# A squared-ReLU attention with an MLP behind it: eight plain block products for the first two chunks, and the weights' sums made later

## Chip, core and metric

One core of one Trainium2 chip. The metric is the device time of one execution in microseconds (us), the median of the runs; lower is better. "PE" is TensorE, "DVE" is VectorE, "ACT" is ScalarE, "POOL" is GpSimd and "SP" is SyncE, which here only issues DMAs.

## What is computed

```python
# u, v: (4, 3008, 256); z: (4, 3008, 64); w_in: (256, 2048); w_out: (2048, 256)
scores = (1.0 / S) * np.matmul(z, z.transpose(0, 2, 1))
attn = np.maximum(scores, 0.0) ** 2
x = (u * np.matmul(attn, v)).reshape(12032, 256)
h = x @ w_in
g = h * np.clip(h + 3.0, 0.0, 6.0) / 6.0
out = g @ w_out
```

The two weights arrive as 64-bit floats; the kernel turns them into 32-bit floats itself.

## The kernel before

**Precision.** Each operand of a matmul is split into a rounded part ("hi", made by a copy on ACT) and the rest ("lo", a subtraction on DVE). A product is three matmuls: lo x hi, hi x lo and hi x hi.

**Attention.** There are 24 chunks of 512 tokens (the last of each batch has 448), and in each 12 pairs of key blocks, so 288 pairs, counted by `g`. A direct pair has 4 matmuls of scores, a mirrored pair has none: it reads a transposed tile that was stored earlier (`turn`, line 374, a DVE transpose). Then come 12 matmuls with `v` (`av`, line 525). The scores run two pairs ahead of `av`: in pair `g` the kernel makes `ah` and `al` of pair `g + 2` (`scores`, line 424). `square_on` says who squares the second copy of the scores: "aa" ACT alone, "dd" DVE alone, "da" half each.

**MLP.** It works on two chunks at a time (12 such couples, `i`), in 8 units each (`q`, 256 columns of `w_in`). Unit `m` starts at pair `g = 33 + 3m` (`MLP_FROM`, `EVERY`) and is spread over three pairs. `group` (line 692) projects up with seven block products by Strassen's scheme (in Winograd's form), 21 matmuls, with sums of blocks of `x` (`split_x`, line 568) and of `w_in` (`S1` to `S4`). It collects them in the PSUM banks `x` and `y`, the ones that the scores use too. Copies on ACT and additions on DVE put the results together, then come ReLU (ACT), `gate` (DVE) and the split into `gh` and `gl`. The unit's down projection is 24 matmuls (`downs_of`, line 623), issued during the next unit.

**The weights.** `weight_ops` (line 796) is a generator. For each of 16 weight blocks it fetches 512 KB, converts it with six DVE instructions (`to_f32`, line 136), makes for `w_in` four sums of blocks (`pieces`, line 171), lets ACT round them, subtracts (`finish`, line 198) and stores hi and lo in DRAM. A step runs up to its next `yield`; an "in" and an "out" block together have 20 steps. `build_rate` (line 816) sets the steps for each pair: 2 for pairs 2 and 3, 1 up to 11, 3 up to 17, 4 up to 32, then 5. `spare()` in the main loop takes one step at a time, at fixed places between the other instructions.

**Order.** The order of every queue is the order of the program (`manual_schedule`); each engine works through its own list and waits where an operand or a buffer isn't ready. `split_x(0)` runs one step a pair from pair 24 to 32; `fetch_unit` (line 687) loads a unit's weights by SP.

Of the kernel before, what the change touches and what calls it, by code (L numbers as in the profile page):

```python
# [15 lines left out]
P = 128  # L16
CH = 512
# [19 lines left out]


# [1 line left out]
def relu2_attention_then_hswish_mlp(  # L40
# [28 lines left out]
    def f(ap):  # L69
        return ap.bitcast(F32)  # L70
# [34 lines left out]
    def copy_later(out, of):  # L105
        copies.append((now, out, of))
# [61 lines left out]
    dw = {}  # L168
    early = True

    def pieces(kind, w):

        hi, lo = piece_tiles(kind)
        if kind == "out":
            copy_later(hi, w)
            return [(hi, lo, w)]
        s = stg.tile([P, 4, P], F32, tag="stg", name="s4")
        a11, a21 = w[:, 0, :P], w[:, 0, P:]
        a12, a22 = w[:, 1, :P], w[:, 1, P:]
        copy_later(hi[:, A11:A22], w[:, :, :P])  # L180
        copy_later(hi[:, A22], a22)
        add(s[:, 0], a21, a22)
        yield
        sub(s[:, 1], s[:, 0], a11)
        yield
        sub(s[:, 2], a11, a21)
        yield
        sub(s[:, 3], a12, s[:, 1])
        copy_later(hi[:, S1:], s)
        yield  # L190
        return [
            (hi[:, A11:A22], lo[:, A11:A22], w[:, :, :P]),
            (hi[:, A22], lo[:, A22], a22),
            (hi[:, S1:], lo[:, S1:], s),
            hi, lo,
        ]

    def finish(kind, q, parts):
        if kind == "out":
            hi, lo = parts[0][:2]  # L200
        else:
            *parts, hi, lo = parts
        flush_copies(upto=now)
        for h, l, of in parts:
            sub(l, of, f(h))
            yield
        d = dw[kind, q] = dwpool.tile([P, 2, *hi.shape[1:]], F32, tag=f"{kind}{q}", name=f"dw{kind}")
        for k, t in enumerate((hi, lo)):
            nc.sync.dma_start(out=d[:, k], in_=f(t))

    built = []

    def piece_tiles(kind):
        homes = (("wh", "wl"), ("gh0", "gl0"), ("gh1", "gl1")) if early else (("wh", "wl"),)
        tags = homes[len(built) % len(homes)]
        built.append(kind)
        tiles = []
        for tag in tags:
            if tag[0] == "g":
                t = gpool.tile([P, 2, CH], F32R, tag=tag, name=tag)  # L220
                t = t.rearrange("p r n -> p (r n)")
            else:
                t = wpool.tile([P, 7 * P], F32R, tag=tag, name=tag)
            if kind == "in":
                tiles.append(t[:, :7 * P].rearrange("p (m f) -> p m f", m=7))
            else:
                tiles.append(t[:, :2 * D].rearrange("p (r d) -> p r d", r=2))
        return tiles

    def fetch_w(kind, q):  # L230
        while (kind, q) not in dw:
            next(w_ops)
        shape = [P, 2, 7, P] if kind == "in" else [P, 2, 2, D]
        if kind == "in":
            t = wring.tile(shape, F32R, tag="wi", name="wi")
        else:
            t = opool.tile(shape, F32R, tag="wo", name="wo")
        nc.sync.dma_start(out=f(t), in_=dw[kind, q])
        return t

    vt, zt = {}, {}
# [326 lines left out]
    def split_x(i):  # L568


        raw = raw_x[i]
        n = tokens(i)[1] // 2
        left, right = raw[:, :, :n], raw[:, :, n:2 * n]
        new = xt[i] = {}

        def piece(k, src):
            shape = [P, 2, CH] if k < 3 else [P, CH]
            homes = ((xpool, f"xh{k}"), (xpool, f"xl{k}"))
            if i == NPR - 1:
# [9 lines left out]
            return lambda: sub(lo, src, f(hi))  # L589

        if i < NPR - 1:
            pool, tag = (rpool, "r") if i else (hpool, "hb")
            t = pool.tile([P, 2, CH], F32, tag=tag, name="t")[:, :, :n]
# [24 lines left out]
        yield  # L618
# [229 lines left out]
    with tc.manual_schedule():  # L848
# [13 lines left out]
        first_scores()  # L862
        run(second, 1)
        split_z(0, 1)
        g_done = 2
        to_fetch += [(b, c, p) for b, c, p in pairs if is_mirrored(b, c, p)]
        for i, (b, c) in enumerate(chunks):
            ahead = b + 1 if c == NCH - 1 and b + 1 < B else None
            for p in range(NPAIR):
# [171 lines left out]
    return a.reshape(2, -1).T.reshape(-1)  # L1041


def _orders():
# [13 lines left out]
    return of_u, of_y  # L1058
# [35 lines left out]
```

## Time and profile before

| | |
|---|---|
| median of 3 runs | 1823.61 us (1823.44 to 1826.42) |
| the profiled execution: its own time, and the span of its instructions | 1825.48 us, 1823.7 us |
| PE, weight loads, DVE, ACT busy | 99%, 87%, 83%, 66% of the span |
| granted TensorE clock | 1.000 (2.4 GHz) |
| DMA | 329.5 MB, mean 181 GB/s |

A matmul's record is about 0.38 us long, but the next one starts 0.22 us later: records overlap, and a PE that is "busy" may still have lost time. The time lost in a stretch is its length less the number of its matmuls times their distance. DVE and ACT records overlap their successors by some hundredths of a microsecond.

### The profile page before, as it was taken

The numbers are of one execution on the slowest core, as the hardware profiler recorded it, in microseconds if no ns is written. First come the engines' busy times: TensorE is split into PE (matmuls) and PEld (weight loads), VectorE is DVE, ScalarE is ACT, GpSimd is POOL, SyncE is SP. The second block draws the span as 40 slices with busy tenths as digits, with TensorE's granted clock in tenths as the row PEclk, the third lists the DMA queues.
The fourth block names the chain that finished last, engine by engine and source line by source line (L and its number), as shares of the span: only waits on it lengthen the run. The fifth ranks groups of instructions, "written<-read, shape, count | busy, mean of one in ns | idle before, by whom it ended". The sixth has DMA issues, their size and how long they took to land.

```text
span 1823.7 us, 23332 instructions
## 1 busy us (share of the span) xinstructions
PE 1798.2 (99%) x8426; PEld 1583.0 (87%) x8426; DVE 1505.6 (83%) x1767; ACT 1198.2 (66%) x1640; POOL 71.9 (4%) x112
## 2 busy tenths in 40 slices
PE   8998999999999999999999999999999999999999
PEld 7877888888998888988899888888889988889888
DVE  8999989888778788997877877888877787887776
ACT  7896656767656555676766655667676565565565
POOL 1000000100000000120000000011000000000000
PEclk9999999999999999999999999999999999999999
DMA  8878888755565667865665668695565667676343
GB/s 224 233 231 257 215 207 199 201 172 176 182 158 165 170 158 172 228 172 182 188 182 136 176 170 173 156 240 176 153 211 142 169 181 173 147 180 168 115 164 127
DMA packets 440627, 329.50 MB, mean 181 GB/s; under 512 B 278848, under 2 KB 397696, under 8 KB 440512
## 3 DMA queue, kind: packets, MB, share of 16 engines
q1 hardware_dynamic: 429952, 292.88, 59.7%
q0 software_dynamic: 10560, 35.13, 6.6%
q8 instruction: 66, 1.08, 0.3%
q14 instruction: 49, 0.40, 0.1%
HBM read 241.70 MB, written 86.25 MB: 180 GB/s over the span
## 4 chain that ended last, share of the span: by engine, by line
PE 74%; DVE 9%; issue 7%; DMA 5%; ACT 4%; SPq 1%; POOL 0%; DVEq 0%; ACTq 0%; POOLq 0%
PE o L73 29%; PE y L73 21%; PE m L73 18%; PE s L73 6%; DMA vraw<-in_v_dram 2%; DVE al L88 2%; DMA zraw<-in_zz_dram 1%; DVE gl L88 1%; DMA l<-d 1%; DVE rb L714 1%; ACT rt L441 1%; DVE r L462 1%; DVE hb L91 1%; ACT gh L774 1%; DMA wi<-dwin 1%
## 5 line engine op out<-in xcount | busy, mean ns | idle before, releaser
L73 PE MATMUL m<-xh,wi 128*128 128x512 f32 (+1 forms) x1344 | 475.7, 377 | 8.0 <-DVE hb L91 4.4
L73 PE MATMUL o<-ah,vl 128*128 128x512 f32 (+1 forms) x1152 | 432.2, 375 | 2.8 <-DVE vl L88 2.1
L73 PE MATMUL o<-ah,vh 128*128 128x512 f32 (+1 forms) x1152 | 431.2, 375 | 0.0
L73 PE MATMUL y<-gh,wo 128*128 128x512 f32 (+1 forms) x1536 | 388.6, 375 | 2.0 <-ACT gh L774 2.0
L73 PE MATMUL o<-al,vh 128*128 128x512 f32 (+1 forms) x1104 | 327.9, 375 | 3.2 <-DVE al L88 3.2
L73 PEld LDWEIGHTS y<-gh,wo 128*128 128x128 f32 x1536 | 289.9, 189 | 37.5 <-ACT gh L774 3.5
L73 PEld LDWEIGHTS m<-xh,wi 128*128 128x128 f32 x1344 | 253.9, 189 | 48.3 <-DVE hb L91 9.2
L73 PE MATMUL m<-xl,wi 128*128 128x512 f32 (+1 forms) x672 | 251.8, 375 | 0.0
L73 PEld LDWEIGHTS o<-ah,vl 128*128 128x128 f32 x1152 | 217.5, 189 | 33.1 <-DVE vl L88 4.2
L73 PEld LDWEIGHTS o<-ah,vh 128*128 128x128 f32 x1152 | 217.7, 189 | 26.7
L73 PEld LDWEIGHTS o<-al,vh 128*128 128x128 f32 x1104 | 208.1, 189 | 30.0 <-DVE al L88 5.7
L73 PE MATMUL y<-gl,wo 128*128 128x512 f32 (+1 forms) x768 | 226.4, 376 | 0.9 <-DVE gl L88 0.5
L441 ACT ACTIVATE rt<-s 128x512 f32<-128x512 f32 (+1 forms) x310 | 180.2, 594 | 70.0 <-PE s L73 64.3
L462 DVE TENSOR_TENSOR r<-rt 128x1024 f32<-128x1024 f32 (+2 forms) x128 | 147.5, 1152 | 80.9 <-ACT rt L441 80.7
L755 ACT ACTIVATE ra<-m,three 128x512 f32<-128x512 f32 (+1 forms) x96 | 65.1, 679 | 174.7 <-PE m L73 134.3
L91 DVE TENSOR_TENSOR hb<-hb,m 128x512 f32<-128x512 f32 (+1 forms) x192 | 128.8, 671 | 59.3 <-PE m L73 58.6
L88 DVE TENSOR_TENSOR al<-r,ah 128x1024 fp32r<-128x1024 f32 (+3 forms) x147 | 164.5, 1119 | 5.2 <-ACT r L460 3.4
L469 ACT ACTIVATE ah<-rt 128x1024 fp32r<-128x1024 f32 (+1 forms) x155 | 163.9, 1057 | 5.0
L73 PEld LDWEIGHTS y<-gl,wo 128*128 128x128 f32 x768 | 144.7, 189 | 20.6 <-DVE gl L88 3.6
L88 DVE TENSOR_TENSOR gl<-rb,gh 128x1024 fp32r<-128x1024 f32 (+2 forms) x97 | 115.4, 1190 | 57.1 <-ACT gh L95 56.6
L88 DVE TENSOR_TENSOR al<-rm,ah 128x1024 fp32r<-128x1024 f32 (+1 forms) x132 | 155.5, 1178 | 1.3 <-ACT ah L408 0.9
L381 DVE STREAM_TRANSPOSE rm<-l 128x1024 f32<-128x1024 f32 (+2 forms) x132 | 149.5, 1133 | 0.1
(87 smaller groups left out, 2190.4 us busy)
## 6 DMA issues: line engine op xcount, KB each, us to landing
wi<-dwin SPq DMA_DIRECT2D x96, 896.0 KB, 5.3
d<-r SPq DMA_DIRECT2D x212, 256.0 KB, 3.2
wo<-dwout SPq DMA_DIRECT2D x96, 512.0 KB, 5.9
l<-d SPq DMA_DIRECT2D x304, 128.0 KB, 3.7
l<-d SPq DMA_DIRECT2D x160, 112.0 KB, 4.8
u<-in_ut_dram POOLq DMA_DIRECT2D x18, 512.0 KB, 4.6
vraw<-in_v_dram POOLq DMA_DIRECT2D x33, 256.0 KB, 4.6
out_dram<-y SPq DMA_DIRECT2D x16, 512.0 KB, 4.0
```

Of the source, the lines that this page charges most:

```text
L73: nc.tensor.matmul(out, lhsT=lhsT, rhs=rhs, start=start, stop=stop, skip_group_check=part)
L88: nc.vector.tensor_tensor(out=out, in0=a, in1=b, op=ALU.subtract)
L91: nc.vector.tensor_tensor(out=out, in0=a, in1=b, op=ALU.add)
L381: nc.vector.transpose(out=rn[:, :, :n].rearrange("p r (k e) -> p r k e", e=32), in_=t[:, :n // 32].rearrange("p k (r e) -> p r k e", r=2),)
L441: nc.scalar.activation(out=halved(rn[:, r]), in_=unpaired(s[:, :n]), func=AF.Relu, scale=1.0 / S)
L462: nc.vector.tensor_tensor(out=to, in0=of, in1=of, op=ALU.mult)
L469: nc.scalar.activation(out=hn, in_=rn, func=AF.Square)
L714: nc.vector.scalar_tensor_tensor(out=out, in0=out, scalar=6.0, in1=h, op0=ALU.min, op1=ALU.mult)
L755: nc.scalar.activation(out=ra[:, 1], in_=c21, func=AF.Relu, bias=three)
L774: nc.scalar.copy(out=ga[0], in_=ra)
```

## The change

- For `i == 0` (units 0 to 7) `group` computes eight plain block products, two for each of four sums: 24 matmuls, no copies out of PSUM, no additions on DVE; each sum goes from PSUM through ReLU (ACT) to `gate` (DVE), which reads the PSUM sum again. `split_x(0)` only splits (5 steps from pair 28, not 9 from pair 24).
- `pieces` and `finish` no longer make sums: they round and split the block and store the float block as well (`dsum`). From pair 49 on, three pairs for each `q`, POOL loads that block back, DVE makes the four sums in place, ACT rounds, DVE subtracts, and SP stores them behind the plain blocks. Units 0 to 7 load four blocks, the later ones seven.
- `build_rate` gives 1 step for pairs 2 to 11, 2 up to 32, then 4; an "in" and an "out" block have 14 steps.
- For chunk 2, DVE squares half ("da") where ACT squared all.
- `w_in` comes with the first half's column blocks swapped, so that the stored blocks stand in the order A21, A11, A12, A22.

```diff
-SPLIT_FROM = 24
+SPLIT_FROM = 28
+SUMS_FROM = 49
-A11, A12, A22, S1, S2, S3, S4 = range(7)
+A11, A12, A22, S3, S2, S4, S1 = range(7)
...
+    def pieces(kind, q, w):
         hi, lo = piece_tiles(kind)
+        copy_later(hi, w)
+        return hi, lo, w
     def finish(kind, q, parts):
+        hi, lo, w = parts
         flush_copies(upto=now)
+        if kind == "in":
+            dsum[q] = dwpool.tile([P, 2, D], F32, tag=f"sum{q}", name="dsum")
+            nc.sync.dma_start(out=dsum[q], in_=w)
+        sub(lo, w, f(hi))
+        yield
...
+    def load_sums(q):
+        t = wpool.tile([P, 2, D], F32, tag="wf", name="s4")
+        nc.gpsimd.dma_start(out=t, in_=dsum[q])
+        summed[q] = t
+    def make_sums(q):
+        t = summed.pop(q)
+        a21, a11, a12, a22 = (t[:, k, m:m + P] for k in range(2) for m in (0, P))
+        add(a22, a21, a22)
+        sub(a21, a11, a21)
+        sub(a11, a22, a11)
+        sub(a12, a12, a11)
+        yield
+        hi, lo = (wpool.tile([P, 2, D], F32R, tag=tag, name=tag) for tag in ("wh", "wl"))
+        nc.scalar.copy(out=hi, in_=t)
+        yield
+        sub(lo, t, f(hi))
+        for k, t in enumerate((hi, lo)):
+            t = t.rearrange("p r (m f) -> p (r m) f", f=P)
+            nc.sync.dma_start(out=dw["in", q][:, k, 4:], in_=f(t))
+        yield
...
+        if i == 0:
+            ra, sums = temp("ra"), {}
+            def part(h, r, k):
+                if k == 0:
+                    sums[h, r] = bank((x_bank, y_bank)[r])
+                o = sums[h, r]
+                a = ((1, 2), (0, 3))[r][k]
+                xh, xl = (paired(x) for x in xt[0][2 * h + k])
+                mm(o, w[:, 1, a], xh, k == 0, False, True)
+                mm(o, w[:, 0, a], xl, False, False, True)
+                mm(o, w[:, 0, a], xh, False, k == 1, True)
+            def relu(out, h, r):
+                nc.scalar.activation(out=out[:, r], in_=sums[h, r], func=AF.Relu, bias=three)
+            part(0, 0, 0)
+            yield
+            part(0, 1, 0)
+            part(0, 1, 1)
+            relu(ra, 0, 1)
+            yield
+            gate(ra[:, 1], sums[0, 1])
+            part(0, 0, 1)
+            relu(ra, 0, 0)
+            late.append(lambda: gate(ra[:, 0], sums[0, 0]))
+            yield
+            part(1, 0, 0)
+            yield
+            part(1, 1, 0)
+            rb = temp("rb")
+            yield
+            part(1, 0, 1)
+            relu(rb, 1, 0)
+            yield
+            gate(rb[:, 0], sums[1, 0])
+            part(1, 1, 1)
+            relu(rb, 1, 1)
...
     def build_rate(g):
-        return 0 if g < 2 else 2 if g < 4 else 1 if g < 12 else 3 if g < 18 else 4 if g < MLP_FROM else 5
+        return 0 if g < 2 else 1 if g < 12 else 2 if g < MLP_FROM else 4
...
-square_on="da" if i < 1 else "aa" if i < 4 else "dd"
+square_on="da" if i in (0, 2) else "aa" if i < 4 else "dd"
```

## Rows read from the trace of the kernel before

**Rows 1.** The page's first part: busy time of each engine.
```profile
PE 1798.2 (99%) x8426; PEld 1583.0 (87%) x8426; DVE 1505.6 (83%) x1767; ACT 1198.2 (66%) x1640; POOL 71.9 (4%) x112
```

**Rows 2.** Table by windows: length, busy PE, PEld, DVE, ACT, POOL, clock, DMA share, GB/s.
```profile
54.75:87.60 32.85, 32.85 (x153) 28.64 (x152) 30.45 (x46) 28.44 (x39) 2.17 (x3) 1.00 0.79 202
87.60:130.20 42.60, 39.58 (x176) 32.24 (x175) 41.80 (x64) 40.71 (x58) 3.62 (x5) 1.00 0.71 229
130.20:162.30 32.10, 26.81 (x117) 21.12 (x116) 31.37 (x50) 23.06 (x33) 2.19 (x3) 1.00 0.89 287
162.30:233.60 71.30, 69.73 (x317) 58.88 (x316) 68.32 (x99) 47.52 (x67) 2.89 (x4) 1.00 0.84 223
...
288.40:384.50 96.10, 94.72 (x453) 85.03 (x452) 84.53 (x102) 66.64 (x96) 14.35 (x22) 1.00 0.79 205
```

**Rows 3.** Timeline of PE at 401 us: start, duration, line, what.
```profile
401.14 0.38 PE L73 MATMUL o<-ah,vl 128*128 128x512 f32 x1
401.35 0.38 PE L73 MATMUL o<-ah,vh 128*128 128x512 f32 x1
```

**Rows 4.** Waits of PE from 87.6 to 130.2: total us, times, longest.
```profile
PE o L73 <- DVE al L88: 2.4, 4, 1.0
```

**Rows 5.** Waits of PE from 130.2 to 162.3 us.
```profile
PE m L73 <- DVE hb L91: 1.7, 1, 1.7
```

**Rows 6.** Timeline of DVE at 93 us.
```profile
92.83 0.69 DVE L88 TENSOR_TENSOR wl<-t,wh 128x512 fp32r<-128x512 f32 x1
93.44 0.29 DVE L91 TENSOR_TENSOR s<-t 128x128 f32<-128x128 f32 x1
```

**Rows 7.** Groups of DVE from 87.6 to 130.2: total busy us, mean ns.
```profile
L158 DVE SCALAR_TENSOR_TENSOR wraw<-wraw 128x512 f32<-128x512 uint32 x5 | 4.5, 897 | 0.2
L149 DVE SCALAR_TENSOR_TENSOR t<-wraw,t 128x512 uint32<-128x512 uint32 x5 | 4.1, 822 | 0.0
L162 DVE SCALAR_TENSOR_TENSOR t<-wraw,t 128x512 f32<-128x512 f32 x4 | 3.2, 804 | 0.1
L153 DVE TENSOR_SCALAR wraw<-wraw 128x512 uint32<-128x512 uint32 x5 | 2.8, 555 | 0.1
L88 DVE TENSOR_TENSOR xl<-u,xh 128x1024 fp32r<-128x1024 f32 x2 | 2.4, 1214 | 0.0
L141 DVE TENSOR_SCALAR t<-wraw 128x512 uint32<-128x512 uint32 x4 | 2.0, 488 | 0.0
L145 DVE TENSOR_SCALAR t<-t 128x512 uint32<-128x512 uint32 x4 | 1.9, 485 | 0.1
...
L88 DVE TENSOR_TENSOR wl<-s,wh 128x512 fp32r<-128x512 f32 x1 | 0.7, 684 | 0.0
...
L88 DVE TENSOR_TENSOR wl<-t,wh 128x256 fp32r<-128x256 f32 x1 | 0.4, 412 | 0.0
```

**Rows 8.** Groups of DVE from 50 to 250 us: total busy us, mean ns.
```profile
L91 DVE TENSOR_TENSOR hb<-hb,m 128x512 f32<-128x512 f32 x12 | 8.2, 680 | 0.0
...
L714 DVE SCALAR_TENSOR_TENSOR rb<-rb,hb 128x1024 f32<-128x1024 f32 x6 | 7.3, 1210 | 0.0
...
L714 DVE SCALAR_TENSOR_TENSOR ra<-ra,m 128x512 f32<-128x512 f32 x6 | 4.1, 680 | 0.1
...
L462 DVE TENSOR_TENSOR r<-rt 128x512 f32<-128x512 f32 x2 | 1.4, 678 | 0.0
```

**Rows 9.** Groups of ACT from 130 to 250 us: total busy us, mean ns.
```profile
L469 ACT ACTIVATE ah<-rt 128x1024 fp32r<-128x1024 f32 x9 | 9.6, 1062 | 0.3
L460 ACT ACTIVATE r<-rt 128x1024 f32<-128x1024 f32 x7 | 7.3, 1046 | 0.5 <-DMA d<-r 0.5
...
L755 ACT ACTIVATE ra<-m,three 128x512 f32<-128x512 f32 x6 | 4.1, 686 | 8.6 <-PE m L73 8.6
```

**Rows 10.** Timeline at 144 us: two DMA issues of the weights.
```profile
144.28 0.73 POOL L127 DMA_DIRECT2D wraw<-in_w_out_dram  x1 [6.99 <-DVE t L162]
...
144.85 0.43 SPq L209 DMA_DIRECT2D dwin<-wh  x1
```

More of the change, by code (lines that the diff above doesn't have):

```diff
@@ L169, in relu2_attention_then_hswish_mlp @@
     early = True
-    def pieces(kind, w):
+    def pieces(kind, q, w):
         hi, lo = piece_tiles(kind)
[L174 to L182, printed above, removed]
-        yield
-        sub(s[:, 1], s[:, 0], a11)
+        copy_later(hi, w)
+        return hi, lo, w
@@ new lines, in finish @@
+    def finish(kind, q, parts):
+        hi, lo, w = parts
+        flush_copies(upto=now)
+        if kind == "in":
+            dsum[q] = dwpool.tile([P, 2, D], F32, tag=f"sum{q}", name="dsum")
+            nc.sync.dma_start(out=dsum[q], in_=w)
+        sub(lo, w, f(hi))
+        yield
+        shape = [P, 2, 8, P] if kind == "in" else [P, 2, 2, D]
+        d = dw[kind, q] = dwpool.tile(shape, F32, tag=f"{kind}{q}", name=f"dw{kind}")
+        for k, t in enumerate((hi, lo)):
+            if kind == "in":
+                t = t.rearrange("p r (m f) -> p (r m) f", f=P)
+                nc.sync.dma_start(out=d[:, k, :4], in_=f(t))
+            else:
+                nc.sync.dma_start(out=d[:, k], in_=f(t))
@@ L185, in pieces @@
+    dsum, summed = {}, {}
+    def load_sums(q):
[9 more added lines that the diff above has]
+        sub(a12, a12, a11)
         yield
-        sub(s[:, 2], a11, a21)
+        hi, lo = (wpool.tile([P, 2, D], F32R, tag=tag, name=tag) for tag in ("wh", "wl"))
+        nc.scalar.copy(out=hi, in_=t)
@@ L187, in pieces @@
         yield
-        sub(s[:, 3], a12, s[:, 1])
-        copy_later(hi[:, S1:], s)
+        sub(lo, t, f(hi))
+        for k, t in enumerate((hi, lo)):
+            t = t.rearrange("p r (m f) -> p (r m) f", f=P)
+            nc.sync.dma_start(out=dw["in", q][:, k, 4:], in_=f(t))
         yield
[L191 to L209, printed above, removed]
@@ L220, in piece_tiles, with fetch_w @@
                 t = gpool.tile([P, 2, CH], F32R, tag=tag, name=tag)
-                t = t.rearrange("p r n -> p (r n)")
+                t = t.rearrange("p r n -> p (r n)")[:, :2 * D].rearrange("p (r d) -> p r d", r=2)
             else:
[L223 to L227, printed above, removed]
+                t = wpool.tile([P, 2, D], F32R, tag=tag, name=tag)
+            tiles.append(t)
         return tiles
-    def fetch_w(kind, q):
+    def fetch_w(kind, i, q):
         while (kind, q) not in dw:
             next(w_ops)
-        shape = [P, 2, 7, P] if kind == "in" else [P, 2, 2, D]
         if kind == "in":
-            t = wring.tile(shape, F32R, tag="wi", name="wi")
-        else:
-            t = opool.tile(shape, F32R, tag="wo", name="wo")
-        nc.sync.dma_start(out=f(t), in_=dw[kind, q])
+            t = wring.tile([P, 2, 7, P], F32R, tag="wi", name="wi")
+            if i:
+                nc.sync.dma_start(out=f(t), in_=dw[kind, q][:, :, 1:])
+            else:
+                nc.sync.dma_start(out=f(t[:, :, :4]), in_=dw[kind, q][:, :, :4])
+        else:
+            t = opool.tile([P, 2, 2, D], F32R, tag="wo", name="wo")
+            nc.sync.dma_start(out=f(t), in_=dw[kind, q])
         return t
@@ L589, in piece @@
             return lambda: sub(lo, src, f(hi))
+        if i == 0:
+            for k, src in enumerate((left, right)):
+                low = piece(k, src)
+                yield
+                low()
+                yield
+            raw_x.pop(i)
+            return
         if i < NPR - 1:
-            pool, tag = (rpool, "r") if i else (hpool, "hb")
-            t = pool.tile([P, 2, CH], F32, tag=tag, name="t")[:, :, :n]
+            t = rpool.tile([P, 2, CH], F32, tag="r", name="t")[:, :, :n]
         else:
@@ L688, in fetch_unit @@
         if m + 1 < NPR * NFP:
-            wi[m + 1] = fetch_w("in", (m + 1) % NFP)
-        wo[divmod(m, NFP)] = fetch_w("out", m % NFP)
+            wi[m + 1] = fetch_w("in", *divmod(m + 1, NFP))
+        wo[divmod(m, NFP)] = fetch_w("out", *divmod(m, NFP))
     def group(m, x_bank="x", y_bank="y"):
@@ L721, in g_tiles, with rest @@
             return gh[:, :, :n], gl[:, :, :n]
+        if i == 0:
+            ra, sums = temp("ra"), {}
[32 more added lines that the diff above has]
+            relu(rb, 1, 1)
+            ga = g_tiles(0)
+            nc.scalar.copy(out=ga[0], in_=ra)
+            yield
+            gate(rb[:, 1], sums[1, 1])
+            sub(ga[1], ra, f(ga[0]))
+            yield
+            gb = []
+            def rest():
+                gb.extend(g_tiles(1))
+                split(*gb, rb)
+            late.append(rest)
+            downs.extend(downs_of(i, q, (ga, gb)))
+            yield
+            return
         end = m == NPR * NFP - 1
@@ L808, in weight_ops @@
                 yield from finish(*before)
-            before = kind, q, (yield from pieces(kind, w))
-        for _ in range(12):
+            before = kind, q, pieces(kind, q, w)
+        for _ in range(8):
             yield
@@ L864, in relu2_attention_then_hswish_mlp @@
         split_z(0, 1)
+        sums = iter(())
         g_done = 2
@@ L888, in relu2_attention_then_hswish_mlp @@
                 if g + 2 < len(pairs):
-                    nxt = scores(*pairs[g + 2], square_on="da" if i < 1 else "aa" if i < 4 else "dd", banks="xy" if at_mlp < 0 else "yx" if on == 2 else "yy")
+                    nxt = scores(*pairs[g + 2], square_on="da" if i in (0, 2) else "aa" if i < 4 else "dd", banks="xy" if at_mlp < 0 else "yx" if on == 2 else "yy")
                 else:
@@ L899, in spare @@
                     weight_work(n)
+                if g > SUMS_FROM and (g - SUMS_FROM) % EVERY == 0:
+                    run(sums, 1)
                 def background():
@@ L984, in relu2_attention_then_hswish_mlp @@
                     xs = split_x(0)
-                if SPLIT_FROM <= g < SPLIT_FROM + 9:
+                if SPLIT_FROM <= g < SPLIT_FROM + 5:
                     run(xs, 1)
-                if g in (SPLIT_FROM + 8, SPLIT_FROM + 16):
-                    load_u(1, g == SPLIT_FROM + 16)
+                if g in (SPLIT_FROM + 4, SPLIT_FROM + 12):
+                    load_u(1, g == SPLIT_FROM + 12)
+                at_sums, of_sums = divmod(g - SUMS_FROM, EVERY)
+                if 0 <= at_sums <= NFP:
+                    if of_sums == 0:
+                        run(sums, 1)
+                        if at_sums < NFP:
+                            load_sums(at_sums)
+                            sums = make_sums(at_sums)
+                    elif of_sums == 2:
+                        run(sums, 1)
                 if done > 1 and since in range(1, 4):
@@ L1041, in _paired, with _swapped @@
     return a.reshape(2, -1).T.reshape(-1)
+def _swapped(w):
+    import numpy as _np
+    w = _np.asarray(w).reshape(2, P, NFP, 2, P)
+    return _np.stack([w[0, :, :, ::-1], w[1]]).reshape(D, DFF)
 def _orders():
```

4 lines of the change are left out of this document (2 added, 2 removed).

## The prediction, made before the changed kernel was run

> **What bounds the kernel now.** I read the page's engine line first: PE is busy 99% of the span, its weight loads 87%, DVE 83% [rows 1]. By that line alone 24 more matmuls are a plain loss. So the next question is whether any stretch exists in which PE isn't the limit, and the table by windows answers it. I cut it where pairs end: pairs 12 to 21, 22 to 32, 33 to 37, 38 to 48, and 58 to 73 [rows 2]. A matmul follows the last one after 0.215 us, as 401.14 and 401.35 show; I use 0.216 [rows 3]. Then the five windows need 153, 176, 117, 317 and 453 matmuls times 0.216 (the last has many narrower ones, so there I take busy PE). That is 33.0, 38.0, 25.3 and 68.5 us of 32.9, 42.6, 32.1 and 71.3: nothing lost in the first, then **4.6, 6.8 and 2.8 us lost**, 14.2 together. The counts include matmuls that reach over an edge, so up to 0.4 is missing from each; I take 15.0.
>
> In these three stretches DVE is busy 41.80 of 42.60, 31.37 of 32.10 and 68.32 of 71.30 us, that is 98, 98 and 96%; in the first one it is at 93% and PE loses nothing [rows 2]. The waits name the same engine: `av` waits for `al` (four times, up to 1.0 us) and a product of a unit for `hb` (1.7 us) [rows 4, 5]. So for some 145 us the kernel is DVE-bound, and time lost there comes back if DVE has less to do.
>
> **What the change costs on PE.** Eight units have 24 matmuls up in place of 21: 8 x 3 x 0.216 = **+5.2 us**, all on the path, since PE is the limit wherever DVE isn't.
>
> **What it takes from DVE.** A 512-wide subtraction is 0.69 us long, but its successor starts 0.61 after it [rows 6]; so I take 0.08 off each duration. The conversion's six instructions are 0.90 + 0.82 + 0.80 + 0.56 + 0.49 + 0.49 = 4.05, less 6 x 0.08, 3.6 us a block [rows 7]. Rounding rests cost 0.61 for "out"; for "in" before 0.61 + 0.34 + 0.21 and four sums of 0.21, 2.0 [rows 6, 7]. So an "in" and an "out" block together took 9.8 us in 20 steps; after the change they take 2 x (3.6 + 0.61) = 8.4 us in 14.
> - Pairs 22 to 32. Before, 44 steps, 2.2 x 9.8 = 21.5 us; after, 22 steps, 22/14 x 8.4 = 13.2: -8.3. `split_x(0)` had four 512-wide operations, three 1024-wide rests (1.13) and a 512-wide one, 6.5 us; two 1024-wide ones stay: -4.2 [rows 7]. "da" adds half a square (0.60) for each of nine direct pairs: +5.4 [rows 8]. Sum -7.1: DVE goes from 41.8 to 34.7 against 37.6 us of PE, 92%.
> - Pairs 33 to 37. The weights: 25 steps, 12.2 us, become 20 steps, 12.0. A unit loses three additions (3 x 0.60) and pays 0.1 more for four half gates (0.60 each) than for two halves and a whole one (1.13) [rows 8]: -1.7 a unit, and 1 2/3 units lie here, -2.8. "da" adds two squares, +1.2. Sum -1.8: 29.6 us of DVE against 25.3 + 5 x 0.216 = 26.4 of PE. DVE **stays over PE here**, since unit 0 has no down projection to fill PE.
> - Pairs 38 to 48. 45 working steps (22 us) become 40 (24 us), as the thinner plan reaches further back: +2. Units: 3 2/3 x -1.7 = -6.2. Sum -4.2: 64.1 us against 68.5 + 11 x 0.216 = 70.9, 90%.
>
> **What loss is left.** The first and third of these come to the level of pairs 12 to 21, 93% and no loss. The bound from above is the row of pairs 38 to 48, 96% and 2.8 lost in 71.3: 1.6 and 3.0 us. I take 0.4 and 0.6, near the lower row. In pairs 33 to 37 DVE wants 29.6/0.98 = 30.2 us, 3.8 more than PE: that is the upper end. The lower is 0.5, because DVE now comes in without a backlog and `al` is made two pairs ahead, which lets it fall behind by a pair before `av` waits; the units' banks leave less. I take 2.0. So 3.0 us are left of 15.0: **-12.0** (ends -6.6 and -14.5).
>
> **What the moved sums cost.** In pairs 51 to 73 each `q` adds four sums and a rest, 4 x 0.21 + 0.61 = 1.45 us of DVE, 0.6 us of ACT, a load on POOL (0.73 to issue) and two stores on SP (0.43 each; with `dsum` 24 more issues on SP in all, 8 on POOL) [rows 6, 10]. Up to pair 57 the plain units give back more than that. In pairs 58 to 73 some 5.4 of them, 7.8 us, meet DVE at 84.5 of 96.1 [rows 2]: 92.3, 96%. By the first window's row that costs nothing, by that of pairs 38 to 48 it makes 4% of 96 us, 4.2, against 1.4 idle now, +2.8. I take **+1.5**, the middle. The queues cost nothing: POOL is busy 14 of these 96 us, a `q` is stored at least one pair before SP fetches it, and that fetch runs a whole unit ahead of its use. The thinner plan forces nothing early either: a block is stored at call 15 + 7n, unit m starts after 52 + 12m calls and needs 29 + 14m, which holds up to m = 11.
>
> ACT isn't a new bound: in pairs 22 to 32 it is at 40.7 of 42.6 [rows 2], and loses nine half squares (some 0.5 of 1.05 each) [rows 9], besides the copies that rounded the omitted pieces of `x` and of the weights; that alone brings it below 90%. The startup up to pair 11 I leave at nothing: one step a pair runs there before and after, except pairs 2 and 3, which lose one each (ends -1 and +0.5).
>
> **The sum:** +5.2 - 12.0 + 1.5 = -5.3 us. The profiled execution took 1825.5, its span 1823.7; the median of the runs, 1823.6, lies 1.9 below it. I move the median by the sum: **1818.3 us**. The ends give -9.3 - 1.0 and +1.4 + 0.5, 1813.3 to 1825.5.
>
> **Rivals.**
> - *DVE still bounds the units.* The conversions are all still there, 2.4 us a pair beyond pair 33, and pairs 33 to 37 stay at more than 100%. If the backlog made there is carried through pairs 38 to 48, only the 4.6 of the first stretch and about 1 come back, and the sums cost 2.8: +5.2 - 5.6 + 2.8 = +2.4; with half of the 9.6 later loss back it is -1.4. So 1822 to 1826. For it: 29.6 against 26.4. Against it: 90% right behind.
> - *Slower, by the handover of bank y.* In a plain unit the first sum is finished by six matmuls in a row, then ACT's ReLU (0.69), then DVE's gate (0.68) must pass before the next pair's scores may write bank y [rows 8, 9]. Three products' matmuls and a down projection cover it, 9 x 0.216 = 1.9 us. On ACT the ReLU stands behind `ah` and a square (1.06 + 1.05), on DVE the gate stands behind an `al` (1.2) and a conversion step (0.8) [rows 7, 9]. Before, one addition did it, straight after three matmuls. If DVE is later than about half a microsecond at that place, each unit stalls by 0.69 + 0.68 + 1.2 + 0.8 - 1.9 = 1.5; eight units 12 us: -5.3 + 12 = +6.7, 1830. Against it: only where the pairs whose scores are made in the unit's first and second pair are both direct is bank y wanted so soon, in units 0 and 4.
> - *The gaps are not DVE's to give.* PE is the most occupied engine, and if its gaps come from fixed chains (a matmul's end, ACT, DVE, PE) rather than from DVE's amount of work, nothing returns: +5.2, 1828.8. The nearness of loss and DVE's excess speaks against it: 93% no loss, 96% 2.8, 98% 11.4 [rows 2]. The Trainium skill (Perfetto Trace Analysis, Identifying the Most-Contended Engine) says to find the engine with the highest occupancy, PE here by its loads too, and optimize that one first; by it work added to PE to relieve DVE makes the kernel 5.2 us slower.
>
> **How the numbers follow.** A measurement tells about 0.2% (3.6 us) from no change. The forecast proper, 1814 to 1820, has 0.64. The first rival, with the weak end of the forecast, is the case "same", 0.24. Slower by over 0.2%, that is above 1827.3, are the handover (0.07) and the fixed chains (0.05). The range 1813.3 to 1824.0 takes in the forecast with its unknown bounds and most of the first rival.
>
> **What would show it.** In the changed trace PE has 24 matmuls more. In pairs 22 to 32 DVE is near 92% and the waits of `av` for `al` are gone; in pairs 33 to 37 two or three microseconds of waits are left, and behind them hardly any; in pairs 58 to 73 DVE is near 96% and the loss 1 to 4 us. Wrong would be: waits of scores for `ra` or `rb` in every unit (the handover), DVE below 95% with the gaps still there (fixed chains), or new waits of PE for `wi`.

## The result and the profile after

The changed kernel takes **1841.47 us** (median of 5 runs, 1840.44 to 1843.21), before 1823.61 (5 runs, 1823.37 to 1826.42): ratio 1.0094, interval 1.0084 to 1.0105. It is 17.9 us slower. The profiled execution took 1843.04, its span 1841.3. Ahead of everything else, the page's engine line [rows 1]:

```profile
PE 1805.4 (98%) x8450; PEld 1590.7 (86%) x8450; DVE 1497.3 (81%) x1748; ACT 1179.6 (64%) x1614; POOL 76.1 (4%) x120
```

There are 24 matmuls more, as foreseen, and DVE and ACT have less to do, as foreseen. PE fell to 98%: it idles more. Where it idles is in the table by windows, with the stretches and columns of [rows 2] and one more, 233.6 to 288.4:

```profile
54.75:87.60 32.85, 32.85 (x154) 28.77 (x153) 27.11 (x33) 27.90 (x36) 2.17 (x3) 1.00 0.83 205
87.60:130.20 42.60, 42.34 (x197) 36.73 (x195) 39.91 (x52) 37.51 (x57) 2.89 (x4) 1.00 0.67 211
130.20:162.30 32.10, 26.44 (x113) 22.28 (x114) 27.70 (x40) 15.19 (x22) 2.17 (x3) 0.95 0.81 237
162.30:233.60 71.30, 67.89 (x311) 58.20 (x310) 61.77 (x81) 39.90 (x53) 4.17 (x6) 1.00 0.75 206
233.60:288.40 54.80, 50.12 (x218) 42.51 (x217) 36.34 (x46) 22.23 (x29) 1.09 (x2) 0.94 0.75 180
288.40:384.50 96.10, 89.60 (x423) 78.23 (x422) 86.46 (x119) 66.03 (x96) 13.62 (x21) 1.00 0.78 215
```

The second stretch has 197 matmuls, 42.6 us by 0.216: nothing is lost any more. The third has 113, 24.4 of 32.1 us: 7.7 lost, although DVE is down to 86%, and the clock column shows 0.95. The fifth, in which DVE is at 66%, loses 7.7 as well (218 matmuls). Before, the same stretch held 256 matmuls and lost nothing, with DVE at 86%:

```profile
233.60:288.40 54.80, 54.80 (x256) 47.80 (x255) 47.06 (x52) 33.63 (x44) 0.00 (x0) 1.00 0.76 188
```

So gaps have come where DVE has time to spare. The waits of PE over the whole run say who holds it:

```profile
PE m L74 <- DVE ra L730: 6.1, 4, 3.9
PE s L74 <- DVE ra L730: 4.5, 2, 3.3
PE m L74 <- ACT hb L814: 2.8, 3, 1.2
PE y L74 <- DVE gl L89: 2.6, 1, 2.6
```

L730 is `gate`, and `m` and `s` are sums of a unit and scores that want a bank which a gate has yet to read. The third line lies in pairs 58 to 73, the last in pair 36; both come up below. In the windows of [rows 4, 5] no wait for a gate was among those on which I built.

Since the changed kernel runs ahead in places, a fixed window no longer holds the same pairs. So I took from each trace the time at which the last `av` matmul of a pair ends, and subtracted that of before:

| pairs | predicted, us | measured, us |
|---|---|---|
| up to 21 (startup) | 0 | -1.7 |
| 22 to 32 | -4.5 | -4.9 |
| 33 to 37 | -4.0 | +2.3 |
| 38 to 48 | -0.1 | +3.1 |
| 49 to 57 | +1.7 | +10.6 |
| 58 to 73 | +1.5 | +7.9 |
| 74 to the end | 0 | +0.7 |

(The predicted column spreads the 5.2 us of matmuls over pairs 33 to 56, 0.216 a pair. What a stretch cost is here and below a difference of times rounded to 0.1 us.) The change does what it should up to pair 32, and from pair 33 on it loses in every stretch until pair 73.

### The profile page after: what moved, and what is told of

It is laid out like the page before. It is cut to its first block, busy times and chain, and to the rows that moved or that the text cites. A ratio compares the mean times of both kernels' runs of the same rounds, so it can differ in the third digit from the quotient of the medians.

```text
span 1841.3 us, 23436 instructions
## 1 busy us (share of the span) xinstructions
PE 1805.4 (98%) x8450; PEld 1590.7 (86%) x8450; DVE 1497.3 (81%) x1748; ACT 1179.6 (64%) x1614; POOL 76.1 (4%) x120
## 4 chain that ended last, share of the span: by engine, by line
PE 70%; DVE 9%; issue 4%; ACT 4%; DMA 3%; SPq 1%; POOL 0%; DVEq 0%; ACTq 0%; POOLq 0%
PE o L74 26%; PE y L74 20%; PE m L74 18%; PE s L74 5%; DVE al L89 1%; DVE gl L89 1%; DVE r L471 1%; DMA wi<-dwin 1%; DVE ra L730 1%; DVE rm L390 1%; DVE rb L730 1%; SPq L351 1%; DVE hb L92 0%; ACT rt L450 0%; DMA zraw<-in_zz_dram 0%
## 5 line engine op out<-in xcount | busy, mean ns | idle before, releaser
L74 PE MATMUL m<-xh,wi 128*128 128x512 f32 (+1 forms) x1360 | 481.0, 378 | 12.2 <-DVE ra L730 6.1
L471 DVE TENSOR_TENSOR r<-rt 128x1024 f32<-128x1024 f32 (+2 forms) x139 | 154.9, 1114 | 84.0 <-ACT rt L450 81.2
L89 DVE TENSOR_TENSOR al<-r,ah 128x1024 fp32r<-128x1024 f32 (+3 forms) x152 | 170.5, 1122 | 11.2 <-ACT r L469 8.0
L92 DVE TENSOR_TENSOR hb<-hb,m 128x512 f32<-128x512 f32 (+1 forms) x176 | 117.6, 668 | 56.7 <-PE m L74 55.4
L825 ACT ACTIVATE ra<-m,three 128x512 f32<-128x512 f32 (+1 forms) x88 | 59.6, 677 | 159.0 <-PE m L74 118.5
```

Of the source, the lines that this page charges most:

```text
L74: nc.tensor.matmul(out, lhsT=lhsT, rhs=rhs, start=start, stop=stop, skip_group_check=part)
L471: nc.vector.tensor_tensor(out=to, in0=of, in1=of, op=ALU.mult)
L825: nc.scalar.activation(out=ra[:, 1], in_=c21, func=AF.Relu, bias=three)
```

## Where the time went

**The handover.** Pair 34, the first unit. DVE's timeline, then PE's:

```profile
129.29 0.69 DVE L471 TENSOR_TENSOR r<-rt 128x512 f32<-128x512 f32 x1
129.89 0.68 DVE L163 SCALAR_TENSOR_TENSOR t<-wraw,t 128x512 f32<-128x512 f32 x1
130.49 0.68 DVE L89 TENSOR_TENSOR wl<-t,wh 128x512 fp32r<-128x512 f32 x1
131.09 0.68 DVE L89 TENSOR_TENSOR al<-r,ah 128x512 fp32r<-128x512 f32 x1
131.78 0.69 DVE L89 TENSOR_TENSOR ah<-r,ah 64x512 fp32r<-64x512 f32 x1
132.50 1.28 DVE L730 SCALAR_TENSOR_TENSOR ra<-ra,m 128x512 f32<-128x512 f32 x2
```
```profile
133.25 0.48 PE L74 MATMUL s<-zy,zx 128*128 128x512 f32 x1 [3.31 <-DVE ra L730]
```

ACT had done its part by then:

```profile
129.36 1.30 ACT L753 ACTIVATE ra<-m,three 128x512 f32<-128x512 f32 x2
```

Both ReLUs end at 130.66, and DVE comes to the gates 1.8 us later. It isn't idle and waits for nothing: the two gates simply stand behind a half square, a conversion step and three subtractions. PE waits 3.3 us, though the scores need only the first of two gates that take 1.28 together. Pair 55 is the same with bank `x`:

```profile
273.14 0.69 DVE L730 SCALAR_TENSOR_TENSOR ra<-ra,m 128x512 f32<-128x512 f32 x1 [1.89 <-ACT ra L753]
273.75 0.28 DVE L92 TENSOR_TENSOR s<-s 128x128 f32<-128x128 f32 x1
274.07 0.94 DVE L89 TENSOR_TENSOR s<-s 128x128 f32<-128x128 f32 x3
274.93 0.68 DVE L89 TENSOR_TENSOR t<-u 128x512 f32<-128x512 f32 x1
275.64 0.69 DVE L89 TENSOR_TENSOR u<-u 128x512 f32<-128x512 f32 x1
276.37 0.69 DVE L89 TENSOR_TENSOR t<-u 128x512 f32<-128x512 f32 x1
276.98 1.22 DVE L89 TENSOR_TENSOR xl<-u,xh 128x1024 fp32r<-128x1024 f32 x1
278.23 0.69 DVE L89 TENSOR_TENSOR u<-u,t 128x512 f32<-128x512 f32 x1
278.84 0.68 DVE L730 SCALAR_TENSOR_TENSOR ra<-ra,m 128x512 f32<-128x512 f32 x1
```
```profile
279.57 0.80 PE L74 MATMUL m<-xh,wi 128*128 128x512 f32 x1 [3.95 <-DVE ra L730]
280.16 0.63 PE L74 MATMUL m<-xl,wi 128*128 128x512 f32 x1
280.59 0.63 PE L74 MATMUL m<-xh,wi 128*128 128x512 f32 x1
```

Between the gate of one row and the gate of the other (`late`) stand the four new sums and five instructions of `split_x(1)`, 5.1 us. Before, ACT copied three of a unit's four results out of bank `x`, and a gate on DVE was the last reader of the fourth alone.

**The clock.** The last two lines above are 0.43 apart, not 0.22. Windows of PE's clock, columns as in [rows 2]:

```profile
145.30:148.70 3.40, 3.40 (x9) 2.67 (x10) 3.12 (x5) 1.49 (x2) 0.00 (x0) 0.50 0.65 231
278.40:285.30 6.90, 5.73 (x14) 4.55 (x15) 3.45 (x5) 0.00 (x0) 0.54 (x1) 0.51 0.59 129
```

The granted clock is 0.50 here, 1.2 GHz in place of 2.4. The first stretch begins right behind a wait of PE that ends at 145.20, the second within the stall of pair 55. Half of 3.4 and of the 5.7 us in which the second one works are lost, some 4.6 us by this estimate. In the rows of before the clock is 1.00 [rows 2].

**A buffer.** The wait that ends at 145.20 is none for a bank. DVE was late with `gl`, the rest that the down projection reads, and some microseconds before it had waited itself, for a buffer whose old content (`d<-r`, a stored square) was still on its way to DRAM:

```profile
138.33 0.69 DVE L471 TENSOR_TENSOR r<-rt 128x512 f32<-128x512 f32 x1 [2.68 <-DMA d<-r]
```
```profile
145.20 1.12 PE L74 MATMUL y<-gl,wo 128*128 128x512 f32 x2 [2.62 <-DVE gl L89]
```

L471 is the half square that the change gave to DVE.

**The sums.** From 295 to 400 us, in pairs 58 to 73, the waits of ACT have a new first line; its first one of before is below it:

```profile
ACT wh L212 <- DVE s L89: 9.8, 6, 2.2
```
```profile
ACT gh L774 <- DVE ra L714: 6.8, 6, 1.9
```

The rounding of a `q` (L212) stands in ACT's queue ahead of copies that empty banks, and waits there for DVE's sums. ACT's timeline shows one, with the copy out of a bank right behind it:

```profile
339.34 0.62 ACT L212 CAST wh<-s 128x512 fp32r<-128x512 f32 x1 [1.94 <-DVE s L89]
339.87 0.58 ACT L814 COPY hb<-m 128x512 f32<-128x512 f32 x1
```

These were readings of the trace. The experiments take them apart.

## The experiments

Time of a pair's end less that of before (whose pair 37 ends at 162.3 us), in us, from the profiled executions. Each of these lies up to 2.1 us from the median of its kernel (the changed kernel's 1.6 above, that of experiment 9 1.3 below), so the table tells where time goes, and the medians tell how much:

```
pair        11    21    32    37    48    57    73   285
after     -1.6  -1.7  -6.6  -4.3  -1.2  +9.4 +17.3 +18.0
1  e1     -1.4  -1.4  -6.4  -4.0  -0.8  +1.9  +8.7  +9.4
2  e2     -1.3  -1.4  -6.3  -4.0  -0.7  +8.9 +12.2 +13.1
3  e3     -1.8  -1.9  -6.8  -4.2  -1.0  +6.5 +13.4 +15.7
4  e4     -1.6  -1.6  -6.2  -5.4  -2.2  +7.4 +14.4 +15.1
5  f1     -1.7  -1.7  -6.7  -7.0  -6.8  -5.0  +2.5  +3.1
6  f2     -1.7  -1.8  -6.8  -7.0  -6.8  -5.0  -1.3  -0.7
7  f3     -1.1  -1.0  -6.0  -5.3  -5.0  -3.2  +0.6  +1.2
8  f4     -0.5  +0.6  +5.3 +12.9 +12.1 +22.3 +29.9 +30.8
9  g3     -1.7  -1.8  -6.6 -10.7 -10.4  -8.7  -5.3  -4.4
10 g1     -1.8  -1.7  -5.9 -10.9 -10.6  -8.9  -5.1  -2.3
11 g2     -1.3  -1.3  -5.7 -10.7 -10.4  -8.7  -0.9  -0.8
12 h1     -1.1  -1.2  -6.0 -10.1  -9.8  -7.6  +7.2  +8.3
```

**1. The late gate at once.**

```diff
-late.append(lambda: gate(ra[:, 0], sums[0, 0]))
+gate(ra[:, 0], sums[0, 0])
```

> The plain unit's second gate (ra, row 0), which frees bank x, is issued right behind its ReLU and no longer with the next pair's late work. Handover theory (a PSUM bank of a plain unit waits for a gate that stands behind other work on DVE, and the long stalls halve TensorE's clock for some us): the four stalls of a product on this gate, 0.7, 1.0, 0.9 and 4.1 us in pairs 39 to 55, go, and with the longest the 6.8 us at 1.2 GHz behind it (3.4 us), so about 10 us less than the changed kernel: 1831. Rival theory (DVE simply has too much to do in pairs 33 to 73): the order of two instructions changes nothing, 1841.

Measured: 1834.79 us, 1.0058 (1.0041 to 1.0074). Pairs 49 to 57 cost 2.7 in place of 10.6 us: the stall of pair 55 and the half clock behind it are gone. Up to pair 48 nothing changed; there the gate stands behind `al` wherever it is issued. So the place of the gate in DVE's queue is the cause in pair 55, and this edit is no cure elsewhere.

**2. The rounding of the sums half a unit later** (in the middle of the unit's second pair, no longer ahead of its first).

```diff
-if g > SUMS_FROM and (g - SUMS_FROM) % EVERY == 0:
-    run(sums, 1)
...
+if g > SUMS_FROM:
+    run(sums, 1)
 prepare()
```

> ACT's rounding of a q's sums is issued in the middle of the unit's second pair, not ahead of it. ACT-queue theory (ACT waits about 2 us for DVE's sums at the head of its queue, while the copies that empty the unit's banks stand behind it): the stalls of products on hb and of scores on hb in pairs 64 to 71 mostly go, 4 to 6 us, 1836. Rival theory (DVE has too much to do there): no change, 1841. The handover theory says nothing about it.

Measured: 1839.21 us, 1.0079 (1.0064 to 1.0094). Pairs 58 to 73 cost 3.3 in place of 7.9 us, and ACT's wait is nearly gone:

```profile
ACT wh L212 <- DVE s L89: 1.2, 2, 0.6
```

So an instruction waiting at the head of ACT's queue was the larger part of the sums' cost: 4.6 us between these two executions, 2.3 between the medians. The other 3.3 are left.

**3. The sums without DVE and ACT.** The four additions, the rounding and the rest are dropped, and the loaded block is stored as it is; this leaves out the sums and their split, so it was to price their DVE and ACT work alone.

```diff
-add(a22, a21, a22)
...
-nc.scalar.copy(out=hi, in_=t)
...
-sub(lo, t, f(hi))
-for k, t in enumerate((hi, lo)):
+for k in range(2):
```

> Leaves out the sums and their split: the loaded blocks are stored as they are, so the DMAs stay and DVE and ACT do nothing for the sums. It bounds what the moved sums cost in all. My prediction put that at 1.5 us (1840). The two traces put 7 us in pairs 60 to 73; with the part of the 4.1 us stall in pair 55 that consists of the four sums (1.3 us) it makes 8 to 9 us, 1832. Should the clock's drop behind that stall go as well, 1829.

Measured: 1840.55 us, 1.009 (1.0075 to 1.0105): both expectations missed. POOL's timeline says why:

```profile
329.38 0.55 POOL L199 DMA_DIRECT2D s<-dsum  x1 [17.90 <-DMA dwin<-s]
329.92 1.44 POOL L255 DMA_DIRECT2D vraw<-in_v_dram  x2
```
```profile
ACT vh L96 <- DMA vraw<-in_v_dram: 3.0, 1, 3.0
```

A load of `dsum` now needs a buffer from which the stores still read. It waits 17.9 us at the head of POOL's queue, the loads of `v` stand behind it, and ACT waits 3.0 us for `v` (second fence, waits of ACT from 330 to 340). The edit put a new wait in place of the work it took away, so it doesn't price the sums in pairs 58 to 73. In pair 55 it does tell something: without the four sums ahead of the `late` gate PE waits 2.8 us for it, not 3.95.

**4. ACT squares chunk 2 again.**

```diff
-square_on="da" if i in (0, 2) else ...
+square_on="da" if i < 1 else ...
```

> Chunk 2 squares on ACT alone again (as the kernel before), the rest of the change stays. Handover theory: DVE's backlog at unit 0 is smaller by two or three half squares (0.6 each), so the 3.5 us stall of the scores on the gate in pair 34 shrinks to about 2 us, and the clock's drop at 145 us (1.7 us) may go: 1838 to 1840. Rival theory (ACT was the limit in pairs 22 to 32): ACT goes back to over 90% there and 1 to 3 us of the 6.6 us gained up to pair 32 are lost: 1843.

Measured: 1841.16 us, 1.0091 (1.0076 to 1.0106). Nothing is lost up to pair 32 without DVE's help, and in pairs 33 to 37 it gains a little (+0.8 in place of +2.3). PE waits 2.8 us for the gate of pair 34, not 3.3, so the half squares are part of what stands ahead of the gates there. DVE's wait for the buffer is gone, PE's wait for `gl` shrinks to 1.6 us, and the half clock at 145 us doesn't come. Its median is within 0.3 us of the changed kernel's.

**5. ACT empties the banks.** A copy takes each sum out of its bank; ReLU and one whole gate work on the copy.

```diff
-nc.scalar.activation(out=out[:, r], in_=sums[h, r], func=AF.Relu, bias=three)
+nc.scalar.copy(out=hb[:, r], in_=sums[h, r])
...
+relu(ra, ha)
+late.append(lambda: gate(ra, ha))
```

> In the plain unit ACT copies each sum out of its bank (as the kernel before did), the ReLU and one whole gate a half work on the copy; nothing else changes. DVE's work is the same within 0.2 us a unit, ACT has 1.9 us a unit more. Handover theory: every stall on the gate goes or shrinks to ACT's delay (3.5 us in pair 34 to about 1; 0.7, 1.0, 1.4, 0.9 and 4.1 us later), and the 10 us at 1.2 GHz with them (5 us): 10 to 13 us less than the changed kernel, 1829 to 1831; pairs 38 to 57 then take about what 24 matmuls more ask for (+4 us against the kernel before). Rival theory (DVE has too much to do): no change, 1841.

Measured: **1828.66 us**, 1.0025 (1.0015 to 1.0035), 12.8 us less than the changed kernel, with the same 24 matmuls. No wait for a gate is left among PE's waits from 120 to 300 us. These are all of them:

```profile
PE s L74 <- ACT rt L450: 2.7, 1, 2.7
PE o L74 <- DVE u L573: 1.8, 2, 1.3
```

Pairs 38 to 57 cost 2.0 us in place of 13.7. So the handover is the cause there, and not how much DVE has to do: from 233.6 to 288.4 us DVE is busier than in the changed kernel (43.20 us against 36.34), and PE loses nothing there (257 matmuls in 54.8 us).

**6. Experiments 2 and 5 together.**

> ACT empties the banks, and the rounding of the sums stands in the middle of the unit's second pair. If both causes are right and lie in different pairs (34 to 56, 64 to 71), their gains add: 10 to 13 and 2 to 5 us off 1841, that is 1824 to 1829. If they are one cause (DVE's load), the sum falls short of that.

Measured: 1825.55 us, 1.0006 (0.9996 to 1.0015). The two gains add (12.8 + 2.3 foretold, 15.9 found). One long stall is left, 2.5 us in the first unit. ACT's timeline, and the DMA view from 126 to 134 us (queue, issues, KB each, median us from issue to landing), with the same line for the whole run:

```profile
133.29 1.15 ACT L759 ACTIVATE ra<-hb,three 128x1024 f32<-128x1024 f32 x1 [2.85 <-DMA d<-r]
```
```profile
d<-r SPq DMA_DIRECT2D x3, 256.0 KB, 6.0
```
```profile
d<-r SPq DMA_DIRECT2D x212, 256.0 KB, 3.2
```

The ReLU waits for its output buffer, which a square of an earlier pair still holds while it is stored. Over the whole run such a store lands after 3.2 us (median of 212), here after 6.0. A like wait held DVE in the changed kernel; here ACT meets it.

**7. The same, with a plan that fetches the weights earlier** (3 steps a pair from 12 to 21, 2 up to 37, then 4).

```diff
-return 0 if g < 2 else 1 if g < 12 else 2 if g < MLP_FROM else 4
+return 0 if g < 2 else 1 if g < 12 else 3 if g < 22 else 2 if g < MLP_FROM + 5 else 4
```

> As the last one, and the weight plan takes 3 steps in pairs 12 to 21 (where DVE has room) and 2 up to pair 37, then 4, so that DVE has 2 steps a pair less to do where unit 0 starts and PE has no down projection. My prediction's step holds that DVE stays over PE in pairs 33 to 37 by 3.2 us; ten steps of 0.6 less, 6 us, should then take away nearly all that is lost there: 3 to 4 us below the last kernel, 1821 to 1825. If the loss there is the handover alone, nothing changes against the last kernel.

Measured: 1826.64 us, 1.0011 (1.0002 to 1.0021), a miss. With fewer steps in the way DVE got to the same buffers sooner and waited for them itself (waits of DVE from 130 to 145 us), 4.7 us, and PE stalled for 3.1, with 3.4 us at half clock behind it:

```profile
DVE r L471 <- DMA d<-r: 4.7, 1, 4.7
```

**8. The changed kernel with the plan of before** (3, 4 and then 5 steps a pair from 12 on).

> The changed kernel with the weight plan of the kernel before (2, 1, 3, 4, then 5 steps a pair), so only the plan is undone. DVE-bound theory for pairs 22 to 32: twice the steps there, 22 x 0.6 = 13 us, bring DVE to 47 us against 37.6 of PE, so the 6.6 us won up to pair 32 turn into a loss of 2 to 5; later the blocks are done sooner, which gives some of it back: 1843 to 1850. Rival theory (the gain up to pair 32 comes from the omitted sums of x and of the weights): no more than 1 or 2 us worse, 1842.

Measured: 1855.99 us, 1.0173 (1.0158 to 1.0188). Pairs 22 to 32 lose 4.7 us where the changed kernel gains 4.9. The window from 87.6 to 142 has DVE busy 53.67 of 54.40 us:

```profile
87.60:142.00 54.40, 47.60 (x207) 37.85 (x205) 53.67 (x77) 41.81 (x62) 6.68 (x9) 1.00 0.79 245
```

So DVE's amount of work is what bounds that stretch, as the prediction had it, and the thin plan is what frees it.

**9. Experiment 6 without the buffers' wait.** "da" for chunk 2 only up to pair 31, so that fewer squares sit in those buffers when the first unit starts, and `split_x(0)` from pair 25, so that the next couple's first load of `u` leaves at pair 29 and not at 32.

```diff
-SPLIT_FROM = 28
+SPLIT_FROM = 25
...
-square_on="da" if i in (0, 2) else ...
+square_on="da" if i == 0 or i == 2 and g < MLP_FROM - 1 else ...
...
-if g in (SPLIT_FROM + 4, SPLIT_FROM + 12):
-    load_u(1, g == SPLIT_FROM + 12)
+if g in (SPLIT_FROM + 4, SPLIT_FROM + 15):
+    load_u(1, g == SPLIT_FROM + 15)
```

> As f2_both, but chunk 2's half squares on DVE end with pair 31 (from pair 32 on ACT squares in place, which needs no second buffer), and x of the first couple is split from pair 25, so that the next couple's 512 KB load leaves at pair 29 and not at 32. Buffer theory (at unit 0 ACT's ReLU waits 2.8 us for a buffer whose 256 KB store is still under way, among the loads that start there): the 2.8 us stall in pair 34 and the 3.4 us at 1.2 GHz behind it go, 3 to 4.5 us less than f2_both's 1825.5: 1821 to 1822.5. Rival theory (DVE has too much to do in pairs 33 to 37): no more than the two half squares, 1.2 us: 1824.5.

Measured: **1821.92 us**, 0.9979 (0.9970 to 0.9989) against 1825.10 of before on the same chip: faster than both kernels, by 3.2 and 19.6 us. Neither ACT nor DVE waits for a store (`d<-r`) in the first unit any more; which part of the edit did it was not taken apart. Its windows, in the order of the table after, of the second, third, fourth and last stretch:

```profile
87.60:130.20 42.60, 42.41 (x196) 36.54 (x194) 39.50 (x51) 37.83 (x56) 3.86 (x5) 1.00 0.70 221
130.20:162.30 32.10, 31.18 (x142) 26.78 (x143) 31.73 (x40) 23.34 (x31) 2.18 (x3) 1.00 0.87 251
162.30:233.60 71.30, 69.91 (x324) 60.90 (x324) 61.87 (x72) 46.63 (x61) 3.52 (x5) 1.00 0.84 227
288.40:384.50 96.10, 92.93 (x439) 81.91 (x438) 90.46 (x125) 68.03 (x97) 16.38 (x26) 1.00 0.86 234
```

From 130.2 to 162.3 there are 142 matmuls where the changed kernel has 113, the clock is 1.00, and DVE is at 99%: now its amount of work is the limit again, as far as its share tells, not its queue's order.

**10. The same with the plan of 7.**

> The same change on f3_both_plan (weights 3 steps in pairs 12 to 21, 2 up to pair 37, then 4). Buffer theory: f3_both_plan's 3.5 us stall in pair 36 (DVE waited 4.7 us for a buffer being stored) goes with the clock's drop behind it; with less of DVE's work at unit 0 as well, 1820 to 1821.5, at or below the kernel without the plan. Rival theory (the plan only shifts DVE's work, and pairs 12 to 21 lose what pairs 33 to 37 win): 1 us above it.

Measured: 1821.80 us, 0.9982 (0.9973 to 0.9992). With the buffers free the plan does no harm, and no good.

**11. The sums a pair earlier** (10, and ACT squares chunk 5).

> As g1_buffers_plan, and the four sums stand at the end of a unit's third pair, their rounding in the middle of its first pair, the rest at that pair's end; chunk 5 squares on ACT (it has room, 71%). Queue-order theory (in pairs 64 to 71 the sums' 1.3 us stand on DVE ahead of the additions that empty the unit's banks): the 3.7 us lost there beyond the kernel before shrink to 1 to 2: 1818 to 1819.5. Rival theory (DVE's amount of work there, 94%): only the omitted squares count, about 1 us: 1820.

Measured: 1825.49 us, 1.0005 (0.9995 to 1.0015), a miss: pairs 58 to 73 cost 7.8 us, in experiment 10 they cost 3.8. The edit has two parts, so how much of it is the sums' place and how much chunk 5's squares stays open.

**12. The sums a pair later** (from 9, with their load a pair later too).

> As g3_buffers, and the four sums stand at the end of a unit's second pair, behind the additions that empty its banks, their rounding and rest in its third pair; the block is loaded a pair later too, and SP fetches it right after it is stored. Queue-order theory (moving the sums a pair earlier cost 4 us, since they came ahead of a unit's additions): behind them they cost less, the stalls on hb at 322, 340 and 344 us (0.9 + 0.7 + 0.3 us) go, 1820. Rival theory (what the sums cost is DVE's time in pairs 64 to 71): 1822, no change. Against both, SP might wait for the store at the head of its queue: then waits for l or for wi appear, 1823 or more.

Measured: 1835.38 us, 1.0058 (1.0045 to 1.0072). Pairs 58 to 73 cost 14.8 us. The first line of SP's own waits from 250 to 390 us, and of DVE's in the same stretch:

```profile
SPq L217 <- DVE wl L89: 19.5, 6, 6.4
```
```profile
DVE rm L390 <- DMA l<-d: 8.6, 2, 4.6
```

The store of a sum (L217) stands at SP's head until DVE has made it, with all other issues behind it; in experiment 9 that wait is 5.6 us. The loads of stored tiles (`l`) leave late, and DVE waits 8.6 us for two of them; in experiment 9 it waits for none. This is the case that the expectation's last sentence names. So no place tried is better for the sums than that of 9, where pairs 58 to 73 cost 3.4 us (-8.7 to -5.3).

## Why the prediction was wrong

The range was 1813.3 to 1824.0 and the time is 1841.47; 0.12 stood for slower.

**The steps that held.** PE's +5.2: 24 matmuls more, no doubt. Pairs 22 to 32: -4.9 where -4.5 was foretold, nothing lost, and DVE at 94%, not 98. Experiment 8 shows that it was DVE's amount of work. The startup gave 1.7, more than the end of -1. Pairs 33 to 37 without the handover and the wait for the buffer: experiment 9 loses about 1.4 us in its window (32.1 - 142 x 0.216), near the 2.0 that I took, with DVE at its limit.

**The step that failed: units at "-1.7 a unit" of DVE work, and the handover a rival for "units 0 and 4" alone.** I added up how much DVE has to do, and DVE did have less. But in a plain unit DVE's gate reads the PSUM bank last, and so the bank is freed when DVE's list comes to the gate. PE waited for such a gate in six of the eight units: for bank `y` in units 0 and 4 (3.3 us, and 1.2 ending at 216.1), for bank `x` in units 2, 3 and 6 (0.5 to 0.9 each, ending at 175.9, 196.0 and 257.2) and in unit 7 (3.95, pair 55). My rival had the mechanism and for bank `y` the two right units, but gave it 0.07. It overlooked bank `x`, which ACT's copies used to free three times in four, and the `late` gate, behind which the new sums and `split_x(1)` moved. Experiment 5 gives back 12.8 us of the 17.9.

**Two terms that were missing: the clock and the buffer.** Two stretches at 1.2 GHz went with the waits of 2.6 and 3.95 us, some 4.6 us in all; part of it is in those 12.8, since experiment 5 has only one such stretch, of 3.4 us. Nothing in the rows of before pointed at it: the clock was 1.00 there, and the longest wait of rows 4 and 5 was 1.7 us. And "da" was priced by DVE's time alone, "+1.2" in pairs 33 to 37. But a square that is stored holds its buffer until the store has landed, and DVE (2.7 us in the changed kernel, 4.7 in experiment 7) or ACT (2.85 in experiment 6) waited for it in the first unit. Experiment 9 removes that and ends 3.6 us below experiment 6; in pairs 33 to 37 it gains 4.1 us on the kernel before, where 6 gains 0.2.

**The second step that failed: "the moved sums, +1.5" and "the queues cost nothing".** They cost 7.9 in the profiled execution, with DVE at 90% from 288.4 to 384.5 us, not 96. I weighed DVE's share and the issues on SP and POOL, but not ACT's queue, where the rounding waits 9.8 us for DVE ahead of copies that free banks. Experiment 2 gives 4.6 of them back; the other 3.3 no experiment removed.

Step by step, the way from the changed kernel to that of experiment 9 is 12.8 us for the handover with the half clock that went with it (5), 3.1 for the rounding (6) and 3.6 for the buffers (9). With the three repaired, the change gains 3.2 us, where 5.3 were forecast. That this is close doesn't make the forecast right: it was made for the kernel as it stood, with these waits in it.

**The rivals.** "DVE still bounds the units" falls for the changed kernel: DVE was at 86 and 87% from 130.2 to 233.6 us. "The gaps are not DVE's to give" falls as well: experiments 5, 6, 7, 9 and 10 keep the 24 matmuls and get most gaps back. It did name the kind of chain (a matmul's end, ACT, DVE, PE) of which the handover is one; the change made such chains where there were fewer. The Trainium skill (Perfetto Trace Analysis, Identifying the Most-Contended Engine) has the engine with the highest occupancy optimized first; by that the change costs 5.2 us. The runs don't agree in either direction: it cost 17.9, and with the banks emptied by ACT, the rounding moved and the buffers freed the same matmuls gave a kernel 0.21% faster than before. For the emptying the Trainium skill (TensorEngine Tiling (Array Packing), PSUM Bottleneck) advises to use both ScalarE and VectorE. Here that held only as far as the order of their queues allowed: before, both did it, and PE lost 2.8 us from 162.3 to 233.6; after, both read the banks, with DVE last, and that cost 12.8 us.

**What stays open.** The plain products weren't tried without the moved sums, nor the sums on POOL. Why the half clock followed some waits and not others isn't shown. The 3.4 us that pairs 58 to 73 still cost in the best kernel, and its 1.4 us from 130.2 to 162.3, weren't traced further.

## What to carry to other kernels

When work moves between engines, adding up busy time isn't enough: ask for each PSUM bank and each buffer which instruction frees it, on whose in-order queue that stands, and what stands ahead of it. Empty a bank on the engine that comes to it soonest, even at the price of an extra copy (12.8 us here), and let an instruction that must wait enter its queue late, behind those that free something. A busy engine may be relieved and the kernel still get slower, so a repaired version that keeps the change's idea is worth a run: the same plain products gave 1.0094 and, with three waits removed, 0.9979.

## What was unexpected of the hardware

- Behind a wait of PE of 2.6 us, and from within one of 3.95 on, the granted clock stood at 0.50 for 3.4 and 6.8 us (matmuls 0.43 us apart, not 0.22), though PE had work again. After another wait of 3.3 us (pair 34) it did not fall. In experiment 10 it fell at 779.8 us for 3.4 us, behind a wait of only 1.9 (the windows' line is below). In experiment 9, where no wait of PE is over 1.5 us, it was 1.00 over the span.

```profile
779.80:783.20 3.40, 3.40 (x11) 2.87 (x10) 3.40 (x5) 1.68 (x3) 0.00 (x0) 0.50 0.95 358
```

- 256 KB stores landed after 6.0 us (median of three) in experiment 6 where the median of the run is 3.2, and ACT waited 2.85 us for a buffer; in experiment 7 DVE waited 4.7 us for one.
- One issue that waits holds its whole DMA queue: 17.9 us on POOL in experiment 3 (for a buffer), up to 6.4 us at a time on SP in experiment 12 (for DVE).
